# A flag for a second program: made from a value already in SBUF and loaded by the engines in the midst of the first program, in place of its end

## The chip, the cores and the metric

The kernel runs on one core of a Trainium2 chip, as one launch. The metric is the device time of that launch in microseconds; lower is better. The engines are TensorE (PE, with its weight loads shown apart as PEld), VectorE (DVE), ScalarE (ACT), GpSimd (POOL) and SyncE (SP). SP issues every DMA here. A row that ends in q (SPq, ACTq, PEldq) is an instruction that an engine's sequencer handles by itself: a wait, a register load, a jump, a DMA issue.

## The reference, cut to what matters

```python
scores = q @ k^T / sqrt(64)                  # 4 batches, 12 heads, 448 x 448
scores = cap * tanh(scores / cap)            # cap is an input, 30.0 here
attn   = softmax(scores)
x      = attn @ v                            # 1792 tokens x 768
h = x @ w_in;  x = (h * cos(h)) @ w_out      # 768 -> 2048 -> 768
a = x @ w1; b = x @ w2                       # 768 -> 1024, twice
out = ((a * b) @ w3) @ w_out2                # 1024 -> 1024 -> 768
```

## The kernel before

The kernel holds two programs that compute the same thing. The first, `program(...)`, takes the softmax without subtracting the maximum, which is safe only while |cap| is at most `CAP_MAX` = 40. The second, `program(..., general=True)`, subtracts the maximum. The first always runs; a flag `large` (1 when |cap| > 40) decides at run time whether the second runs after it and overwrites the output. With cap = 30 the flag is 0, and every engine jumps over the second program's instructions to the end of the code.

In each program a planner (`Plan.schedule`) takes operations with costs and due times and writes out one list of instructions for all engines, in the order of its own modelled time `t`; the five engines execute their part of that list in order. Attention comes first (lines 574, 584, 595), then the first MLP with its three-term products of high and low halves (lines 357 to 359, tiles `wih`, `woh`, `xh`, `gh`), then the second MLP (tiles `w12h`, `w34h`, `abh`) whose results leave through the tiles `ob` (three buffers) to `outT`.

The flag before: behind the first program, `tile_kernel` loads cap from HBM once more (line 299, tile `cap2`, shown as `cap`), takes its absolute value and compares it (lines 300 to 302, on DVE), and each of the five engines loads the flag from SBUF into a register (`nc.values_load`, line 303, a TENSOR_LOAD; SP adds a range check of two instructions, FUSED_REGOPS and SEQ_ASSERT). Then each engine executes the jump of `tc.If` (COMPARE_BRANCH, also line 303). These instructions are placed by the framework, not by the planner: each stands on its engine as soon as its inputs allow. In `program`, line 446 already makes `pac` = |cap| in SBUF at the start, on all 128 partitions.

Of the kernel before, what the change touches and what calls it, by code (L numbers as in the profile page):

```python
# [10 lines left out]
F32 = mybir.dt.float32  # L11
# [3 lines left out]
ALU = mybir.AluOpType  # L15
# [18 lines left out]
CAP_MAX = 40.0  # L34
# [255 lines left out]
def tile_kernel(tc, *args):  # L290


    nc = tc.nc
    cap = args[3]
    program(tc, *args)
    with tc.tile_pool(name="large", bufs=1) as p:
        c = p.tile([1, 2], F32, name="cap2")
        large = p.tile([1, 1], mybir.dt.int32, name="large")
        nc.sync.dma_start(c[:, 0:1], cap.rearrange("(o n) -> o n", o=1))
        nc.vector.tensor_scalar(c[:, 1:2], c[:, 0:1], -1.0, None, op0=ALU.mult)  # L300
        nc.vector.tensor_tensor(c[:, 0:1], c[:, 0:1], c[:, 1:2], op=ALU.max)
        nc.vector.tensor_scalar(large, c[:, 0:1], CAP_MAX, None, op0=ALU.is_gt)
        with tc.If(nc.values_load(large[0:1, 0:1], min_val=0, max_val=1) > 0):
            program(tc, *args, general=True)


@with_exitstack
def program(
# [12 lines left out]
    general=False,  # L321
):
    nc = tc.nc
    PE, ACT, DVE, POOL, SP = nc.tensor, nc.scalar, nc.vector, nc.gpsimd, nc.sync
    G = dict(PAR, **GENERAL) if general else PAR
    plan = Plan()
# [76 lines left out]
    def swap(*names, opens=()):  # L403


        def f():
            for n in names:
                pools[n].close()
            for n in opens:
                pools[n].open()  # L410

        plan.event(f, [pools[n] for n in names], [pools[n] for n in opens])
# [21 lines left out]
    def const(shape, name, dtype=F32):  # L434
        return pools["const"].pool.tile(shape, dtype, name=name, bufs=1)
# [8 lines left out]
    pac = const([P, 1], "pac")  # L444
# [5 lines left out]
    warm = const([P, 1], "warm")  # L450
    DVE.memset(warm, 0.0)
    ACT.activation(warm, warm, AF.Tanh)


    xh_r = ring("xring", "xh", [P, KD, S], F32R)
# [657 lines left out]
    swap("wp", opens=("yp", "mp", "cv"))  # L1113
    swap("cv", "attn", opens=("lp",))
    swap("mp", "yp", "wi", opens=("qp", "q2"))
    for _, f in plan.schedule():
        if f is not None:
            f()
    for n in ("q2", "qp", "lp", "psum", "dram", "xring", "const"):
        pools[n].close()  # L1120


# [40 lines left out]
```

## Time and profile before

| | us |
|---|---|
| time, median of three runs (lowest, highest) | 1142.9 (1142.64, 1143.47) |
| time of the profiled execution | 1141.23 |
| its span, first to last instruction | 1139.2 |
| PE busy | 1112.9 |
| DVE busy | 740.5 |
| ACT busy | 454.2 |
| POOL busy | 133.3 |

The span is what the trace covers; 2.03 us of the profiled execution's time lie outside it. PE is busy for 98% of the span, so its few gaps and the tail behind its last matmul are what is left beside its own work.

### The profile page before, as it was taken

The numbers are of one execution on the slowest core, as the hardware profiler recorded it, in microseconds if no ns is written. First come the engines' busy times: TensorE is split into PE (matmuls) and PEld (weight loads), VectorE is DVE, ScalarE is ACT, GpSimd is POOL, SyncE is SP. The second block draws the span as 40 slices with busy tenths as digits, with TensorE's granted clock in tenths as the row PEclk, the third lists the DMA queues.
The fourth block names the chain that finished last, engine by engine and source line by source line (L and its number), as shares of the span: only waits on it lengthen the run. The fifth ranks groups of instructions, "written<-read, shape, count | busy, mean of one in ns | idle before, by whom it ended". The sixth has DMA issues, their size and how long they took to land.

```text
span 1139.2 us, 13718 instructions
## 1 busy us (share of the span) xinstructions
PE 1112.9 (98%) x5184; PEld 966.5 (85%) x5184; DVE 740.5 (65%) x1111; ACT 454.2 (40%) x581; POOL 133.3 (12%) x130
## 2 busy tenths in 40 slices
PE   5999999999999999999999999999999999999997
PEld 3777777778888888889999999998999999999996
DVE  5888777899998897787899877768831311311111
ACT  4887767877566655722454211113211101101001
POOL 2312111123231110110121000001200000000000
PEclk9999999999999999999999999999999999999999
DMA  8885765878756554337745211101401101101001
GB/s 231 229 224 149 212 185 171 231 210 252 209 154 188 190 148 158 130 100 235 272 127 180 70 56 56 29 1 69 140 15 41 57 1 41 57 1 40 10 1 51
DMA packets 83165, 140.10 MB, mean 123 GB/s; under 512 B 35986, under 2 KB 63634, under 8 KB 83090
## 3 DMA queue, kind: packets, MB, share of 16 engines
q1 hardware_dynamic: 83090, 139.14, 40.7%
q8 instruction: 42, 0.69, 0.2%
q14 instruction: 33, 0.27, 0.1%
HBM read 109.45 MB, written 29.58 MB: 122 GB/s over the span
## 4 chain that ended last, share of the span: by engine, by line
PE 93%; DVE 2%; DMA 1%; ACT 1%; SPq 1%; issue 0%; POOL 0%; ACTq 0%; DVEq 0%
PE bank L357 13%; PE bank L358 13%; PE bank L359 13%; PE double L358 12%; PE double L359 12%; PE double L357 12%; PE bank L595 12%; PE double L574 3%; PE double L575 3%; DMA rawc<-in_w_out 1%; SPq L353 1%; DMA kr<-in_k 0%; DVE w L343 0%; ACT double L584 0%; ACT p L584 0%
## 5 line engine op out<-in xcount | busy, mean ns | idle before, releaser
L343 DVE TENSOR_TENSOR a<-double,a 128x448 f32<-128x448 f32 x32 | 20.0, 625 | 240.1 <-PE double L359 237.7
L595 PE MATMUL bank<-p,v 112*128 112x448 f32 x384 | 161.3, 543 | 0.5 <-issue 0.5
L359 PE MATMUL double<-xh,w12l 128*128 128x448 f32 x378 | 137.8, 365 | 0.0
L358 PE MATMUL double<-xl,w12h 128*128 128x448 f32 x378 | 137.8, 365 | 0.0
L357 PE MATMUL double<-xh,w12h 128*128 128x448 f32 x378 | 137.4, 363 | 0.0
L584 ACT ACTIVATE double<-double,ts 112x896 f32<-112x896 f32 x96 | 94.1, 981 | 79.1 <-PE double L575 78.9
L333 ACT COPY a<-double 128x448 f32<-128x448 f32 x31 | 16.5, 533 | 254.1 <-PE double L359 254.1
L357 PE MATMUL bank<-xh,wih 128*128 128x448 f32 x270 | 107.9, 399 | 0.0
L595 PEld LDWEIGHTS bank<-p,v 112*128 112x128 f32 x384 | 72.6, 190 | 41.2 <-issue 38.3
L357 PE MATMUL bank<-gh,woh 128*128 128x448 f32 x260 | 102.1, 393 | 0.3 <-ACT hs L333 0.3
L358 PE MATMUL bank<-xl,wih 128*128 128x448 f32 x270 | 98.3, 364 | 0.0
L359 PE MATMUL bank<-xh,wil 128*128 128x448 f32 x270 | 98.0, 363 | 0.0
L584 ACT ACTIVATE p<-double,pac 112x896 f32<-112x896 f32 x96 | 96.7, 1010 | 2.0
L358 PE MATMUL bank<-gl,woh 128*128 128x448 f32 x260 | 95.2, 366 | 0.0
L359 PE MATMUL bank<-gh,wol 128*128 128x448 f32 x260 | 94.8, 365 | 0.0
L574 PE MATMUL double<-qh,ks 128*112 128x448 f32 x192 | 73.7, 384 | 14.4 <-DVE ks L343 10.3
L343 DVE TENSOR_TENSOR y<-bank,y 128x448 f32<-128x448 f32 x111 | 68.6, 619 | 23.0 <-PE bank L359 22.2
L358 PEld LDWEIGHTS double<-xl,w12h 128*128 128x128 f32 x378 | 71.0, 188 | 5.8
L357 PEld LDWEIGHTS double<-xh,w12h 128*128 128x128 f32 x378 | 70.8, 187 | 5.6
L359 PEld LDWEIGHTS double<-xh,w12l 128*128 128x128 f32 x378 | 71.0, 188 | 5.0
L575 PE MATMUL double<-ql,ks 128*112 128x448 f32 x192 | 72.1, 375 | 0.0
L357 PEld LDWEIGHTS bank<-xh,wih 128*128 128x128 f32 x270 | 50.8, 188 | 9.0 <-issue 5.0
(153 smaller groups left out, 2359.2 us busy)
## 6 DMA issues: line engine op xcount, KB each, us to landing
rawc<-in_w_out SPq DMA_DIRECT2D x16, 768.0 KB, 5.6
rawl<-in_w SPq DMA_DIRECT2D x16, 768.0 KB, 4.4
qr<-in_q SPq DMA_DIRECT2D x48, 224.0 KB, 4.6
kr<-in_k SPq DMA_DIRECT2D x48, 224.0 KB, 4.9
rawc<-in_w_in SPq DMA_DIRECT2D x13, 768.0 KB, 5.0
raw<-in_w3T SPq DMA_DIRECT2D x16, 512.0 KB, 5.8
raw<-in_w_out SPq DMA_DIRECT2D x8, 768.0 KB, 7.2
wo_d<-wx SPq DMA_DIRECT2D x16, 384.0 KB, 4.4
```

Source lines behind the costliest of these rows:

```text
L333: "A": ("ACT", (0.051 if psum else 0.094) + n / 1200, lambda: ACT.copy(dst(), src())),
L343: "D": ("DVE", 0.068 + n / 960, lambda: DVE.tensor_tensor(dst(), a(), b(), op=op))
L353: plan.op(due, [("SP", 0.66, lambda: SP.dma_start(dst(), src()))], r=r, w=w, kb=kb)
L357: PE.matmul(out, wh, xh, start=first, stop=False)
L358: PE.matmul(out, wh, xl, start=False, stop=False)
L359: PE.matmul(out, wl, xh, start=False, stop=last)
L574: PE.matmul(o, w, qh(), start=True, stop=False)
L575: PE.matmul(o, w, ql(), start=False, stop=True)
L584: lambda f=f, x=x, o=o: ACT.activation(o(), s(), f, scale=x[:CP]))],
L595: PE.matmul(pv()[:, :S], w()[:, 2 * c + n].rearrange("p a d -> p (a d)"), p()[:, n, :], start=c == 0 and n == 0, stop=c == NT - 1 and n == 1)
```

## The change

The flag is now made inside the first program from `pac`, as an operation of the planner on DVE with due time 30 and cost 0.15. The five loads of the flag into registers are written out by hand at the first entry of the planner's list with modelled time over 600, and the register is handed back to the caller for the jump. The second load of cap, the absolute value and the tile `cap2` are gone. The jump itself stays where it was, at the end of the first program.

```diff
 def tile_kernel(tc, *args):
-    nc = tc.nc
-    cap = args[3]
-    program(tc, *args)
-    with tc.tile_pool(name="large", bufs=1) as p:
-        c = p.tile([1, 2], F32, name="cap2")
-        large = p.tile([1, 1], mybir.dt.int32, name="large")
-        nc.sync.dma_start(c[:, 0:1], cap.rearrange("(o n) -> o n", o=1))
-        nc.vector.tensor_scalar(c[:, 1:2], c[:, 0:1], -1.0, None, op0=ALU.mult)
-        nc.vector.tensor_tensor(c[:, 0:1], c[:, 0:1], c[:, 1:2], op=ALU.max)
-        nc.vector.tensor_scalar(large, c[:, 0:1], CAP_MAX, None, op0=ALU.is_gt)
-        with tc.If(nc.values_load(large[0:1, 0:1], min_val=0, max_val=1) > 0):
-            program(tc, *args, general=True)
+    with tc.If(program(tc, *args) > 0):
+        program(tc, *args, general=True)
...
     ACT.activation(warm, warm, AF.Tanh)
+
+    if not general:
+        large = const([1, 1], "large", mybir.dt.int32)
+
+        def is_large():
+            DVE.tensor_scalar(large, pac[0:1], CAP_MAX, None, op0=ALU.is_gt)
+
+        plan.op(30.0, [("DVE", 0.15, is_large)])
+    over = None
...
-    for _, f in plan.schedule():
+    for t, f in plan.schedule():
+        if over is None and not general and t > 600:
+            over = nc.values_load(large[0:1, 0:1], min_val=0, max_val=1)
         if f is not None:
             f()
...
+    return over
```

Apart from the rows of the flag, each engine's instructions keep their order. Three places show where those rows go.

ACT at the end of the first program, before. The three copies write the last output tiles; the last row is the first one of the second program.

```order
L333 COPY ob0_6106<-bank6_79 128x448
L333 COPY ob1_6112<-bank4_77 128x448
L333 COPY ob2_6119<-double1_76 128x448
L303 TENSOR_LOAD large_7571
L303 COMPARE_AND_BRANCH
L452 ACT_TABLE_LOAD
```

The same place now:

```order
L323 COPY ob0_6122<-bank6_79 128x448
L323 COPY ob1_6128<-bank4_77 128x448
L323 COPY ob2_6135<-double1_76 128x448
L293 COMPARE_AND_BRANCH
L442 ACT_TABLE_LOAD
```

The register load between the last copy and the jump is gone; PE and DVE lose theirs in the same way. On SP the load already stood far from the end before, behind the second load of cap.

SP in the first MLP, now. The DMAs fetch weights; ISA x2 is the range check. Before, the five DMAs above and the five below stood next to each other.

```order
L343 DMA wx1_1563<-wi_d_85 128x768
L343 DMA xl_1_3975<-w34_d_87 128x768
L343 DMA wx0_1542<-wo_d_86 128x768
L343 DMA rawl1_3847<-in_w12 128x1536
L343 DMA wx1_1563<-wo_d_86 128x768
L1117 TENSOR_LOAD large_103
L1117 ISA x2
L343 DMA wx0_1542<-wi_d_85 128x768
L343 DMA wx1_1563<-wi_d_85 128x768
L343 DMA rawl0_3838<-in_w12 128x1536
```

Three sequencer instructions moved in between the load of `wx1` from `wo_d` and that of `wx0` from `wi_d`.

PE at the same point of the list, now: a pair of products with `gh` ends, one with `xh` begins.

```order
L347 MATMUL bank7_80<-gh0_1635,woh3_1858 128x448
L348 MATMUL bank7_80<-gl0_1644,woh3_1858 128x448
L349 MATMUL bank7_80<-gh0_1635,wol3_1875 128x448
L1117 TENSOR_LOAD large_103
L347 MATMUL bank5_78<-xh0_438,wih2_1349 128x448
L348 MATMUL bank5_78<-xl0_454,wih2_1349 128x448
L349 MATMUL bank5_78<-xh0_438,wil2_1364 128x448
```

The load stands between two matmuls that followed one another before. In the trace of before this point is at 589.9 us, and it lies between 586 and 591 us on the other four engines.

## Rows read from the trace of the kernel before

**Rows 1.** The page's part 1: busy time, share of the span, instructions.

```profile
PE 1112.9 (98%) x5184; PEld 966.5 (85%) x5184; DVE 740.5 (65%) x1111; ACT 454.2 (40%) x581; POOL 133.3 (12%) x130
```

**Rows 2.** PE's waits: in total, times, longest us.

```profile
PE double L358 <- DVE gl L343: 2.6, 1, 2.6
```

**Rows 3.** Stretches: length, busy PE, PEld, DVE, ACT, POOL, granted clock, DMA, GB/s.

```profile
32.00:37.00 5.00, 5.00 (x16) 3.10 (x15) 4.97 (x9) 4.02 (x6) 1.25 (x1) 0.66 0.54 154
...
600.00:700.00 100.00, 100.00 (x496) 92.51 (x495) 82.06 (x131) 25.47 (x35) 7.50 (x6) 1.00 0.29 90
...
770.00:775.00 5.00, 2.42 (x13) 1.87 (x12) 4.55 (x8) 2.45 (x4) 0.00 (x0) 1.00 0.00 0
```

**Rows 4.** Line 303 from 1120 us: ns min/median/max, first and last start.

```profile
L303 SPq EVENT_SEMAPHORE  x8: 17/17/17, 1137.3 to 1137.8; - x8
...
L303 ACTq EVENT_SEMAPHORE  x2: 17/28/38, 1133.0 to 1136.7; - x2
...
L303 PEldq TENSOR_LOAD <-large x1: 490/490/490, 1127.5 to 1127.5; - x1
L303 PEldq COMPARE_BRANCH  x1: 3322/3322/3322, 1128.1 to 1128.1; - x1
L303 ACTq TENSOR_LOAD <-large x1: 550/550/550, 1133.1 to 1133.1; - x1
...
L303 SPq COMPARE_BRANCH  x1: 53/53/53, 1134.3 to 1134.3; - x1
```

**Rows 5.** Last matmul, a late copy on ACT, and the last output DMA.

```profile
1130.86 0.37 PE L359 MATMUL double<-abh,w34l 128*128 128x448 f32 x1
...
1131.62 1.11 ACT L333 COPY ob<-bank 128x448 f32<-128x448 f32 x2 [1.60 <-PEq L303]
...
L353 SPq DMA_DIRECT2D outT<-ob x1: 385/385/385, 1133.8 to 1133.8; - x1
...
DMA to landing us min/median/max: 2.8/2.8/2.8
```

**Rows 6.** Line 303 on SP in the middle of the program.

```profile
L303 SPq TENSOR_LOAD <-large x1: 702/702/702, 492.7 to 492.7; - x1
L303 SPq FUSED_REGOPS  x1: 188/188/188, 493.5 to 493.5; - x1
L303 SPq SEQ_ASSERT  x1: 37/37/37, 493.7 to 493.7; - x1
```

**Rows 7.** SP and DVE in order of time, 486 to 498 us (idle before, releaser).

```profile
486.26 0.45 SPq L299 DMA_DIRECT2D cap<-in_cap  x1
...
492.11 0.13 DVE L300 TENSOR_SCALAR cap<-cap 1x1 f32<-1x1 f32 x1
...
492.62 0.62 DVE L343 TENSOR_TENSOR y<-double,y 128x448 f32<-128x448 f32 x1
...
497.77 0.63 DVE L343 TENSOR_TENSOR y<-double,y 128x448 f32<-128x448 f32 x1 [1.73 <-PE double L359]
```

**Rows 8.** What stands behind the new loads: four engines, 588 to 592 us.

```profile
589.82 0.95 DVE L343 TENSOR_TENSOR wol<-wx,woh 128x768 fp32r<-128x768 f32 x1
...
589.93 0.96 ACT L959 ACTIVATE w<-w 128x896 f32<-128x896 f32 x1 [0.99 <-DVE w L343]
...
591.32 2.55 POOL L337 TENSOR_SCALAR woh<-wx 128x768 fp32r<-128x768 f32 x1 [4.71 <-DMA wx<-wo_d]
...
588.22 0.32 SPq L353 DMA_DIRECT2D wx<-wo_d  x1
590.80 6.88 SPq L353 DMA_DIRECT2D wx<-wi_d  x2
```

**Rows 9.** PE: a wait of its sequencer, and the matmul that it belongs to.

```profile
L357 PEldq EVENT_SEMAPHORE  x1: 51/51/51, 600.9 to 600.9; - x1
...
603.31 0.37 PE L357 MATMUL double<-gh,woh 128*128 128x448 f32 x1
```

**Rows 10.** DVE behind the arithmetic on cap at the start.

```profile
5.92 0.63 DVE L334 CAST qh<-qr 128x896 fp32r<-128x896 f32 x1 [1.66 <-DMA qr<-in_q]
```

## The prediction

> **What bounds the kernel now.** I read the busy shares first, then PE's waits, then the tail. PE is busy for 1112.9 of 1139.2 us [rows 1], so a change off PE's path can only act through a gap of PE or through the tail behind its last matmul. Inside the program the list of PE's waits has one large entry behind the start-up, 2.6 us on DVE's `gl` [rows 2], in the stretch 770 to 775 us, where DVE is busy for 4.55 of 5 us [rows 3]. The reader is to see that PE waits neither for SP nor for a flag anywhere.
>
> The tail decides this change. PE's last matmul runs from 1130.86 to 1131.23; the last output DMA is issued at 1133.8 and lands 2.8 us after that, at 1136.6 [rows 5]. SP jumps at 1134.3, as soon as that issue is done, and its next instruction, the first of eight waits, is at 1137.3 [rows 4]. Those 3.0 us are the jump: by then the DMA has been down for some 0.7 us. From there to the end of the span are 1.9 us of waits, one after another. So the tail hangs on SP: last issue, jump, waits.
>
> **The change part by part.** Everything is set against the profiled execution, 1141.23 us.
>
> *At the end.* PE, DVE and ACT lose their flag loads. On ACT the load takes 0.55 us from 1133.1, right behind the last copy's start, and ACT's own closing wait is over at 1136.7 [rows 4]; without the load and its dispatch ACT arrives some 0.6 us sooner, at 1136.1. It was not last: SP arrives at 1137.3. On PE the load takes 0.49 us at 1127.5 and the jump begins at 1128.1, while matmuls run until 1131.23 [rows 4, 5]; PE's jump lasts until 1131.4, and would again end about when the matmuls do. Gain at the end: 0. What is late next if I misread SP's 3.0 us is the landing of the last DMA, so the most that the tail can give is 1137.3 less 1136.6, 0.7 us.
>
> Would a flag known early make the jump itself cheap? The trace of before already holds that experiment. SP had its flag in a register from 493.7 us on [rows 6], because the framework had moved its load there, and still spent 3.0 us between its jump and the next instruction [rows 4]. ACT, PE and DVE only come to what SP had. The Trainium skill (Runtime: NRT & Kernel Launch, section Instruction fetch mechanics) gives a reason against the change: a taken branch to a target outside the instruction window must wait for a fetch of the target's page. By that rule the jump costs the same with an early flag, the sum has no term for it, and the trace agrees with its 3.0 us on SP. If instead the early flag let the jump be prepared, the sum would gain the 0.7 us above and no more.
>
> *At 486 to 494 us.* SP loses the issue of the second load of cap (0.45 us at 486.26) [rows 7] and a flag load with its range check: from 492.7 to 493.7, 0.70, 0.19 and 0.04 us with the gaps between them [rows 6]. DVE loses three tiny operations: from the first at 492.11 to the next real one at 492.62, 0.5 us. DVE then stands idle for 1.73 us before 497.77, waiting for PE [rows 7]; 0.5 us sooner it waits 0.5 us longer. Bounds: gain between 0 and 0.5 us. I take 0, because that idle time is three times the saving.
>
> *The flag made at the start.* One more DVE operation of a tenth or two of a us, like those on cap (0.13 us for a 1x1 tile [rows 7]). It stands in front of the first cast of `qh`, before which DVE idles for 1.66 us for a DMA [rows 10]. Cost 0; without that cover 0.2 us.
>
> *The five loads in the middle.* The dearest load in the trace is SP's 0.70 us, 1.05 us with its check [rows 6]. I go through what is queued behind each.
> - SP: the DMA in front is issued from 588.22 to 588.54, the one behind at 590.80 [rows 8]. The 1.05 us fit into 2.26 us; 1.2 us are left. The DMA behind waits for others, not for SP.
> - ACT: idle for 0.99 us before the `w` at 589.93, the load 0.55 us [rows 8, 4]. Hidden.
> - POOL: idle for 4.71 us before 591.32 [rows 8]. Hidden.
> - DVE: full there, with `wol` at 589.82 behind the load [rows 8]. At most 0.7 us lost, if the load can't run beside the operation in front. Over the next 100 us DVE is busy for 82 [rows 3], so 18 us can take it up before the one stretch where PE waits for DVE. Between 0 and 0.7 us on DVE; on PE's path I take 0.
> - PE: it is the one that matters, since PE has no idle time there. Its sequencer runs ahead of the array. The load at the end stands behind all matmuls in PE's order, and ran at 1127.5, when the last matmul was 3.4 us off [rows 4, 5]. Nearer to the new place, the wait at 600.9 belongs to the matmul at 603.31 (the only one of that stretch that waits for two engines): 2.4 us ahead [rows 9]. The load holds the sequencer for 0.6 us (1127.5 to 1128.1). Cost 0 with either lead; if the load emptied the array first, 0.6 us and the 0.37 us of a first matmul, 1.0 us. I take 0, since at the end the matmuls ran on beside the load.
>
> The Trainium skill (DMA: Bandwidth & Descriptors, section Latency and other measured facts) gives a floor of about 600 ns for such a register load. The trace has 490, 550 and 702 ns, so two of the three lie below that floor; by that figure the PE term would be the same 0 under a lead of 2.4 us, or 0.6 us if it were exposed.
>
> **Sum.** 0 at the end, 0 at 486 to 494, 0 at the start, 0 in the middle: 1141.23 us for an execution like the profiled one. It lies 1.67 us below the median of the three runs, 1142.9, so for the median I predict **1142.9 us**. Adding the bounds, the program can move between 1.2 us down (0.7 + 0.5) and 1.0 us up. About 0.2% of 1142.9, 2.3 us, is what a measurement of this kernel can tell from no change; neither bound reaches it.
>
> **The rivals.**
> - *The tail shortens* (0.08). For: ACT's copy at 1131.62 has 1.60 us of wait put down to PE's step on line 303 [rows 5], which would move with PE's load; and DVE's 0.5 us could survive. Against: that copy also needs the buffer of the first of six output DMAs, which were under way then. Gain 0.6 to 1.2 us: 1141.7 to 1142.3.
> - *PE waits for its load* (0.05). For: it is the first register load with matmuls behind it, and no row shows that. Against: rows 4 and 5. Cost up to 1.0 us: 1143.9.
> - *PE waits and loses its clock* (0.03), slower than before. After the start-up gaps the granted clock was 0.66 on average over 32 to 37 us, of its levels 2.4 and 1.2 GHz; that is 1.7 us of clock. Against: the 2.6 us gap at 771 was followed by no loss, the granted clock being 1.00 in 770 to 775 [rows 3]. 1.0 + 1.7 = 2.7 us: 1145.6. It decides as soon as the load empties the array and the clock follows once.
> - *The jump pays twice* (0.02): the code behind it lies elsewhere now, and a second wait like SP's 3.0 us would give 1145.9. Nothing in the rows speaks for it.
> - That the change doesn't do what it says is out: the order listing shows the loads where the diff puts them.
> - What I can't name, such as the buffers that lie 32 bytes further on because of the new tile: 0.05 faster and 0.02 slower by more than 0.2%.
>
> **How the numbers follow.** The forecast of no visible change has 0.75; with the first two rivals, which also stay within 0.2%, 0.88. Slower: 0.03 + 0.02 + 0.02 = 0.07. Faster: 0.05. Range: from the lowest run less the gains, 1142.64 - 1.2 = 1141.4, taken down to 1141.0 because the profiled execution itself had 1141.23; up to the highest run and the PE bound, 1143.47 + 1.0 = 1144.5. It leaves out the clock, the double jump and the unnamed, 0.12.
>
> **What the profile of the changed kernel would show.** Right: five TENSOR_LOADs between 586 and 592 us, PE's steps around 590 unbroken, SP's DMA behind its load still at 590.8; no ops of lines 300 to 302 at 492 and a DVE wait before 497.8 that is longer by 0.5 us; at the end ACT's closing wait 0.6 us earlier, SP's jump still followed by 3.0 us. Wrong: a step between two of PE's matmuls of 0.6 us or more at 590, a granted clock under 1.00 behind it, or SP's first wait at the end coming less than 2.5 us after its jump.

## The result, and the profile after

The changed kernel takes 1151.1 us in the median of six runs (1148.6 to 1153.2), against 1143.2 us for the kernel before (six runs, 1142.6 to 1146.1): a ratio of 1.006, with a 95% interval from 1.0045 to 1.0076. It is slower by 7 to 8 us, outside the predicted 1141.0 to 1144.5. The profiled execution has a time of 1148.61 us and a span of 1146.6, 7.4 us more than before.

Nothing that the change was said to touch carries that. The page's part 1 of the changed kernel, to be read against [rows 1]: the same 5184 matmuls, and PE is busy for 7.0 us more, while DVE and ACT have the same busy time within 0.4 us.

```profile
PE 1119.9 (98%) x5184; PEld 967.3 (84%) x5184; DVE 740.7 (65%) x1109; ACT 453.8 (40%) x581; POOL 135.2 (12%) x130
```

PE's largest wait inside the program is the one of [rows 2] still. The list of PE's waits, after:

```profile
PE double L348 <- DVE gl L333: 2.6, 1, 2.6
```

So PE doesn't wait longer; it works longer. Where, a table by stretches shows (length, busy us of PE, PEld, DVE, ACT, POOL with the number of instructions that started, granted clock, DMA share, GB/s). Two stretches in which PE never rests, one in the first MLP and one in the second, and two in which the clock moved (before, 32 to 37 us is in [rows 3]). Before:

```profile
500.00:580.00 80.00, 80.00 (x397) 74.21 (x396) 69.11 (x104) 27.42 (x39) 10.50 (x10) 1.00 0.67 223
770.00:785.00 15.00, 12.42 (x61) 10.98 (x60) 13.46 (x24) 6.02 (x10) 0.00 (x0) 1.00 0.00 0
800.00:1100.00 300.00, 300.00 (x1485) 278.39 (x1484) 76.72 (x123) 34.41 (x61) 6.73 (x6) 1.00 0.11 38
```

After:

```profile
32.00:37.00 5.00, 5.00 (x20) 3.40 (x19) 4.97 (x9) 4.97 (x7) 1.25 (x1) 1.00 0.61 203
500.00:580.00 80.00, 80.00 (x392) 73.34 (x391) 68.62 (x103) 26.97 (x39) 9.26 (x9) 1.00 0.67 220
770.00:785.00 15.00, 12.40 (x54) 11.02 (x54) 12.21 (x22) 5.40 (x9) 0.00 (x0) 0.89 0.00 0
800.00:1100.00 300.00, 300.00 (x1471) 276.28 (x1470) 79.89 (x127) 36.24 (x64) 7.79 (x7) 1.00 0.12 40
```

The reader divides length by matmuls. From 500 to 580 us a matmul takes 80/397 = 0.2015 us before and 80/392 = 0.2041 after; from 800 to 1100 us 300/1485 = 0.2020 and 300/1471 = 0.2039. PE is at 100% in all four and the granted clock is 1.00 in all four. Each matmul has become about 1% longer, with no gap between them. The two stretches stand on either side of the new register loads at 590 us, and the first lies before them, so those loads can't be the cause.

Matching the start of every matmul with that of its counterpart places the 7.4 us. At 206 us, where the first MLP's matmuls set in, the changed kernel is 1.8 us ahead; in 32 to 37 us alone it gained 1.7 us, because its clock did not fall there (1.00 above, 0.66 in [rows 3]). From there to 767 us it loses 5.0 us in small, even steps; 1.2 us around 778 us, where its clock fell (0.89) and that of before did not; 3.3 us in even steps to the last matmul; and the tail is 0.3 us shorter. The even steps are 8.3 us. The two clock events are of opposite sign and cancel for the greater part.

What the prediction did follow is unharmed. The new loads, by line:

```profile
L1117 POOLq TENSOR_LOAD <-large x1: 503/503/503, 587.1 to 587.1; - x1
L1117 PEldq TENSOR_LOAD <-large x1: 488/488/488, 587.9 to 587.9; - x1
L1117 ACTq TENSOR_LOAD <-large x1: 462/462/462, 589.3 to 589.3; - x1
L1117 DVEq TENSOR_LOAD <-large x1: 546/546/546, 590.2 to 590.2; - x1
L1117 SPq TENSOR_LOAD <-large x1: 488/488/488, 590.3 to 590.3; - x1
```

PE in order of time at the place of its load, which stands between the first two of these rows in PE's order:

```profile
591.32 0.36 PE L349 MATMUL bank<-gh,wol 128*128 128x448 f32 x1
591.52 0.37 PE L347 MATMUL bank<-xh,wih 128*128 128x448 f32 x1
591.73 0.37 PE L348 MATMUL bank<-xl,wih 128*128 128x448 f32 x1
```

The load ran at 587.9, 3.6 us before the matmul behind it at 591.52, and the steps around it are 0.20 and 0.21 us. On SP the load fits in front of a DMA that comes no later for it:

```profile
589.89 0.32 SPq L343 DMA_DIRECT2D wx<-wo_d  x1
592.47 6.89 SPq L343 DMA_DIRECT2D wx<-wi_d  x2
```

From the end of the first to the second are 2.26 us, as in [rows 8] to the hundredth. The tail, by line (answers to [rows 4]):

```profile
L293 SPq EVENT_SEMAPHORE  x8: 17/17/17, 1144.7 to 1145.2; - x8
...
L293 SPq COMPARE_BRANCH  x1: 50/50/50, 1141.7 to 1141.7; - x1
L293 ACTq EVENT_SEMAPHORE  x1: 17/17/17, 1142.6 to 1142.6; - x1
```

SP's jump at 1141.7 is followed by the first wait at 1144.7: 3.0 us, as before, and ACT, without its load, is done 2.1 us before SP (0.6 us before it in [rows 4]).

### The profile page after: what moved, and what is told of

It is laid out like the page before. It is cut to its first block, busy times and chain, and to the rows that moved or that the text cites. A ratio compares the mean times of both kernels' runs of the same rounds, so it can differ in the third digit from the quotient of the medians.

```text
span 1146.6 us, 13710 instructions
## 1 busy us (share of the span) xinstructions
PE 1119.9 (98%) x5184; PEld 967.3 (84%) x5184; DVE 740.7 (65%) x1109; ACT 453.8 (40%) x581; POOL 135.2 (12%) x130
## 4 chain that ended last, share of the span: by engine, by line
PE 92%; DVE 2%; DMA 2%; ACT 1%; issue 0%; SPq 0%; ACTq 0%; DVEq 0%
PE bank L347 13%; PE bank L349 13%; PE bank L348 13%; PE double L349 12%; PE double L348 12%; PE double L347 12%; PE bank L594 11%; PE double L573 3%; PE double L574 3%; DMA raw<-in_w_out 2%; DMA kr<-in_k 1%; DVE w L333 0%; ACT double L583 0%; SPq L343 0%; DVE y L333 0%
## 5 line engine op out<-in xcount | busy, mean ns | idle before, releaser
L348 PEld LDWEIGHTS bank<-xl,wih 128*128 128x128 f32 x270 | 50.9, 188 | 9.2 <-issue 5.2
```

The lines of the kernel that those rows point to most:

```text
L348: PE.matmul(out, wh, xl, start=False, stop=False)
```

## The experiments

The suspects were three. **A:** the flag's tile takes 32 bytes in the first pool of SBUF, and 53 buffers behind it, among them `xh` and `xl`, which stream through PE as moving operands in both MLPs, lie 32 bytes further on; their place changes the matmul's step. **B:** the register loads or the flag's DVE operation cost the time. **C:** the clock's fall behind the gap at 771 us.

**Only the 32 bytes.** The kernel before, with

```diff
     warm = const([P, 1], "warm")
+    if not general:
+        const([P, 1], "pad")
```

> The kernel before, with nothing of the change but one unused 32-byte tile at the place in SBUF where the change puts its flag, so that the same 53 buffers lie 32 bytes further on. Theory A (the place of the buffers makes PE's matmuls slower): 1149 to 1152 us, ratio to before 1.005 to 1.007, and a step between PE's matmuls of 0.205 us in the stretch from 500 to 580 us, where before has 0.202. Theory B (the register loads in the middle, or the flag made at the start, cost it): 1143 us, ratio 1.000. Theory C (PE's clock fell once behind the gap near 771 us): 1143 us or, if it falls here too, 1.2 us more.

Measured: 1153.1 us, ratio 1.0076 (1.0051 to 1.0102). An unused tile alone costs as much as the change did, within the two intervals; the time is 1 us above the range expected. Its stretches:

```profile
500.00:580.00 80.00, 80.00 (x392) 73.25 (x391) 68.20 (x104) 26.24 (x38) 9.30 (x9) 1.00 0.64 216
800.00:1100.00 300.00, 300.00 (x1472) 275.97 (x1471) 79.37 (x126) 36.27 (x64) 7.62 (x7) 1.00 0.13 44
```

392 and 1472 matmuls, as in the changed kernel (392, 1471).

**The change without the 32 bytes.** The changed kernel, with the flag in the second word of the tile `warm`, which takes 32 bytes anyway:

```diff
-    warm = const([P, 1], "warm")
+    warm2 = const([P, 2], "warm")
+    warm = warm2[:, 0:1]
...
-        large = const([1, 1], "large", mybir.dt.int32)
+        large = warm2[0:1, 1:2].bitcast(mybir.dt.int32)
```

> The change in full, but the flag lies in the unused second word of the 32 bytes that the tile named warm already takes, so that every other buffer has the address that it had before. Theory A: 1143 us, ratio 1.000 (0.998 to 1.002), PE's steps 0.202 us from 500 to 580 us. Theory B: 1149 to 1152 us, ratio 1.006. Theory C: 1143 us, with no tie to the addresses.

Measured: 1143.8 us, ratio 0.9995 (0.9982 to 1.0007).

```profile
500.00:580.00 80.00, 80.00 (x397) 74.22 (x396) 68.90 (x105) 27.10 (x39) 9.69 (x9) 1.00 0.66 218
770.00:785.00 15.00, 12.39 (x54) 11.03 (x53) 12.15 (x21) 5.17 (x9) 0.00 (x0) 0.89 0.00 0
800.00:1100.00 300.00, 300.00 (x1485) 278.36 (x1484) 79.24 (x126) 35.44 (x62) 7.21 (x7) 1.00 0.12 38
```

397 and 1485: the counts of before. All of the change's instructions are in it, and it costs nothing that can be measured. B falls. C falls with it: the clock fell behind the gap near 771 us in this profile too (0.89 in the second row), and the time is that of before.

**64 bytes.** The changed kernel with the `pad` tile of the first experiment as well.

> The change in full with one more unused 32-byte tile behind the flag, so that the 53 buffers lie 64 bytes further on than before. Theory A with a period of 64 bytes (only the remainder by 64 counts, and it is 32 for all buffers, as before): 1143 us, ratio 1.000. Theory A with a longer period or none: another time, 1145 us or more. Theory B: 1149 to 1152 us, as the changed kernel.

Measured: 1148.3 us, ratio 1.0040 (1.0024 to 1.0057). Not the time of before: the remainder by 64 is not all that counts.

**32 bytes above xh and xl.** The kernel before, with a pool of 32 bytes opened between the pool of `xh` and `xl` and that of attention:

```diff
-    for n in ("const", "xring", "dram", "psum", "attn", "wi", "wp"):
+    for n in ("const", "xring", "gap", "dram", "psum", "attn", "wi", "wp"):
         pools[n].open()
+    pools["gap"].pool.tile([P, 1], F32, name="pad", bufs=1)
```

> The kernel before with 32 unused bytes between the buffers of xh and xl and those of attention and of the early weights of the second MLP: xh and xl stay where they were, the attention buffers and the early w12 and w34 tiles move by 32 bytes. Theory A, if it is the place of xh and xl as the moving operand that counts: 1143 us, ratio 0.999 to 1.001, steps of 0.202 us from 500 to 580 us. Theory A, if it is the place of the attention buffers and the early weights: up to 1150 us. Theory B: 1143 us.

Measured: 1143.0 us, ratio 0.999 (0.9976 to 1.0004). The attention buffers and early weights moved, `xh` and `xl` did not, and the time stayed. So it is the four buffers of `xh` and `xl`; what remained was whether their place counts by itself (A1) or against that of the weights, which PE's weight loads read while the moving operand streams (A2; in the stretch from 500 to 580 us of before, PEld is busy for 74 us beside PE's 80).

**The other side moved instead.** The buffers that grow from the far end of SBUF (`wi`, `wo`, `g`, `y`, most of `w12` and `w34`) were moved by a pool opened first on that side:

```diff
-    for n in ("const", "xring", "dram", "psum", "attn", "wi", "wp"):
+    for n in ("const", "xring", "dram", "psum", "attn", "rgap", "wi", "wp"):
         pools[n].open()
+        if n == "rgap":
+            pools[n].pool.tile([P, 8], F32, name="pad_r", bufs=1)
```

> The kernel before, with xh, xl and all buffers of attention in place, and the buffers on the other side of SBUF (wi, wo, g, y, most of w12 and w34) moved by 32 bytes the other way, so that xh lies 32 bytes further from its weights, as in the changed kernel. Theory A1 (the absolute place of xh and xl counts): 1143 us, ratio 0.998 to 1.002, steps of 0.202 us from 500 to 580 us. Theory A2 (the place of xh and xl relative to the weights that are loaded beside them counts): 1149 to 1153 us, ratio 1.005 to 1.008, steps of 0.205 us.

Measured: 1153.1 us, ratio 1.0080 (1.0063 to 1.0098). `xh` stands exactly where it stood before, and the kernel is as slow as with the pad in front of it.

```profile
500.00:580.00 80.00, 80.00 (x391) 73.23 (x390) 66.58 (x102) 25.99 (x37) 9.40 (x9) 1.00 0.65 217
800.00:1100.00 300.00, 300.00 (x1463) 274.45 (x1462) 78.44 (x125) 36.11 (x63) 8.44 (x7) 1.00 0.13 43
```

**Both sides, 256 bytes in sum.** The pad of 32 bytes of the first experiment, and the pool on the far side with 224 bytes (56 words in place of 8).

> The kernel before with xh, xl and the attention buffers moved by 32 bytes, as in the changed kernel, and the other side moved by 224 bytes the other way, so that the distance between the two grows by 256 bytes. Theory A1 (absolute place): 1149 to 1153 us, ratio 1.005 to 1.008, steps of 0.205 us. Theory A2 with a period that divides 256 bytes: 1143 us, ratio 0.998 to 1.002, steps of 0.202 us; A2 with a longer period: in between or slower.

Measured: 1142.1 us, ratio 0.9984 (0.9971 to 0.9996). `xh` lies where it lies in the changed kernel, and the slowness is gone. A1 falls, and A2 fits all six experiments so far: the distance counts, and 256 bytes more leave it as it was.

```profile
500.00:580.00 80.00, 80.00 (x398) 74.26 (x397) 68.89 (x105) 27.20 (x39) 9.66 (x9) 1.00 0.65 218
800.00:1100.00 300.00, 300.00 (x1485) 278.58 (x1484) 79.74 (x127) 35.32 (x62) 7.75 (x7) 1.00 0.11 38
```

**96 and 128 bytes.** The pad of the first experiment with 24 and with 32 words in place of one.

> The kernel before with 96 unused bytes in front of xh. With 32 bytes the ratio was 1.0076, with 64 (beside the flag) 1.0040. Both forms of theory A with a period of 64 bytes are out already; with a period of 128, 96 bytes is the one offset not yet seen, and any value from 0.998 to 1.010 fits. If the steps depend on the place only through whole multiples of 64 or not, 1150 us as with 32 bytes.

> The kernel before with 128 unused bytes in front of xh. Theory A with a period of 128 bytes (or 32 or 64): 1143 us, ratio 0.998 to 1.002. With a longer period: another time, as 32 and 64 bytes gave.

Measured: 1151.0 us, ratio 1.0060 (1.0041 to 1.0080), and 1147.8 us, ratio 1.0036 (1.0021 to 1.0050). A period of 128 bytes is out as well.

**What the traces of these runs say of the distance.** For each matmul of the MLPs behind attention (from about 495 us on) I took the address of its moving operand and that of the weights loaded next, from the built programs, and their difference modulo 256 bytes. The mean step to the next matmul, by that difference (number of pairs in brackets):

```
difference   0              64            96            128           160           192
before       0.2039 (1716)  0.2021 (151)                                            0.2007 (1241)
changed      0.2040 (1709)                0.2015 (151)                0.2056 (1241)
64 bytes     0.2050 (1709)                              0.2035 (1392)
96 bytes     0.2041 (1718)                0.2062 (1241)               0.2054 (151)
128 bytes    0.2056 (1706)  0.2018 (1241)                                           0.2002 (151)
```

The 1241 pairs of before at 192 are those of `xh` with the weights on the far side. The change put them at 160, the slowest column but one. Where 192 occurs, it is the best column of its row. In the kernel before, more than half of the pairs lie at 0, so there was something to be had.

A pair's own distance is not the whole of it. By the table, with 128 bytes some 1.4 us of the loss come from the large group (192 to 64), but some 2.9 us from the pairs at 0, whose distance did not change. The means at 0 are good to about 0.001 us (0.2031 in the second experiment, which has the addresses of before), so this is more than scatter. Most plainly, the 430 products of `abh` and `abl` with `w34` on the far side, where neither operand moved, step by 0.2057 us there, and by 0.2026 in the kernel before and in the three others with its distances (no shift, both sides, and the last one below). And the 151 pairs at 96 step by 0.2015 us in the changed kernel but by 0.2062 with the other side moved instead, at the same distance. What else these steps depend on is open.

A rival that needs no new run is that the moved buffers collide with other engines or with DMAs. Between 800 and 1125 us, 400 of the 583 pairs at 192 of before ran while DVE, ACT and POOL did nothing and no DMA packet was under way, and so did 380 of the 553 pairs at 160 of the changed kernel. Their mean steps are 0.2003 and 0.2053 us, the same as those of all such pairs there. So the cost is there without any work of the others.

**Every pair at 192.** The flag in the unused word, as in the second experiment, a gap of 192 bytes as in the fourth, and `g` and `ab` placed 64 bytes further inside buffers that are 256 bytes larger:

```diff
+    class Shifted(Ring):
+        def tile(self, k):
+            if k not in self.tiles:
+                n = math.prod(self.shape[1:])
+                t = self.pool.pool.tile([P, n + 64], ...)[:, 16:16 + n]
...
-        g_r = hl("mp", "g", [P, 2, S], 2)
+        g_r = [Shifted(plan, pools["mp"], "g" + x, [P, 2, S], F32R, 2) for x in "hl"]
...
-        ab_r = hl("qp", "ab", [P, S], 2)
+        ab_r = [Shifted(plan, pools["qp"], "ab" + x, [P, S], F32R, 2) for x in "hl"]
```

> The changed kernel with the flag in a word that was unused, and with pads that put every moving operand of both MLPs (xh, xl, g, ab) at the same distance from its weights, 192 bytes modulo 256: a gap of 192 bytes below the attention buffers and early weights, and 64 bytes inside the g and ab buffers. Before, 2122 of 3967 such pairs of matmul and next weight load lay at 0 and stepped by 0.2036 to 0.2043 us, 1694 at 192 with 0.2003 to 0.2011. Theory A2 (the distance counts): some 1006 x 0.0033 + 694 x 0.0032 + 420 x 0.002 = 6 us less than before, 1137 to 1139 us, ratio 0.993 to 0.997, steps under 0.2025 us in both MLPs. If the slow steps of xh come from something else that the pads only happened to move: 1142 to 1144 us or, with the moved g and ab in other bad places, more.

Measured: 1135.1 us, ratio 0.9931 (0.9919 to 0.9944): 8 us less than before, with the change's loads in it and as many instructions as the changed kernel. It is faster than both kernels. The ratio lies in the range expected, the time 2 us below it; the spans of the two profiled executions differ by 6.1 us (1133.1 against 1139.2), which is what the sum had.

```profile
PE 1106.2 (98%) x5184; PEld 967.0 (85%) x5184; DVE 743.7 (66%) x1109; ACT 453.8 (40%) x581; POOL 133.1 (12%) x130
...
500.00:580.00 80.00, 80.00 (x402) 74.84 (x401) 69.70 (x105) 27.85 (x41) 10.52 (x10) 1.00 0.68 225
800.00:1100.00 300.00, 300.00 (x1502) 281.19 (x1501) 76.37 (x123) 35.01 (x62) 6.79 (x6) 1.00 0.11 38
```

402 and 1502 matmuls in the stretches where before had 397 and 1485; 300/1502 = 0.1997 us each.

**The change as it is, with the distance mended.** The changed kernel, flag tile included, and the far side moved by 224 bytes.

> The changed kernel as it is, flag tile and register loads included, with only the buffers of the other side moved by 224 bytes the other way, so that the 32 bytes of the flag become 256 in the distance. Theory A2: 1143 us, ratio 0.997 to 1.001. If the change has a cost of its own beside the distance: more than 1144.5 us, ratio over 1.001.

Measured: 1142.8 us, ratio 0.9992 (0.9983 to 1.0002). The flag tile may stay where it is, if the far side follows.

## Why the prediction was wrong

The step that failed is the prediction's first premise, that a change off PE's path "can only act through a gap of PE or through the tail", and with it a term that the sum does not have. The prediction names it, "the buffers that lie 32 bytes further on because of the new tile", among the things that I could not name a price for, gives it 0.02 for a loss over 0.2%, and leaves it out of the parts of the change. It was the whole result: the first experiment costs 0.76% with that tile alone, the second and the last show the rest of the change at -0.05% and -0.08%, with intervals from -0.18% to 0.07%. What would have warned me was in the trace of before: matmuls of one form that step by different times at a granted clock of 1.00, which no wait explains. In the second MLP the 216 products of `xh` with a `w12h` on the far side step by 0.199 us, the 168 with one of the early `w12h` by 0.204. I read PE as busy at 98% and took its busy time as fixed by the work.

The rest, by its steps:

- *End: gain 0.* Right. SP's jump kept its 3.0 us, and no other engine was later than SP. ACT's arrival moved further ahead of SP's than I said, by 1.5 us in place of 0.6, and it moved nothing. The tail is 0.3 us shorter, within the bound of 0.7.
- *486 to 494 us: gain 0.* Right in size, but not where I put it. DVE's 0.5 us did not lengthen the wait before [rows 7]'s last operation, which stayed (1.75 us, 1.73 before); DVE met a wait of its own at once. DVE in order of time, after:

```profile
493.07 0.62 DVE L333 TENSOR_TENSOR y<-double,y 128x448 f32<-128x448 f32 x1 [0.48 <-PE double L349]
...
498.25 0.62 DVE L333 TENSOR_TENSOR y<-double,y 128x448 f32<-128x448 f32 x1 [1.75 <-PE double L349]
```

- *The loads in the middle: cost 0.* Right on all five engines. PE's lead was 3.6 us, more than the 2.4 I counted on, and the dearest load in the middle took 0.55 us, not the 0.70 taken as the bound.
- *Rivals.* None of them happened as written. "PE waits and loses its clock" ended on the right side for a wrong reason: PE did not wait for its load. Its "against", that the gap at 771 us costs no clock, does not hold: in 8 of the 12 kernels profiled here the clock was halved for 3.4 us or more some microseconds behind that gap, in kernels fast and slow alike. Six of the eight falls began behind 775 us, where the row that I read ends; the one profiled execution of the kernel before has none.
- *Range.* Its bounds were those of the waits that I had listed, and so could not hold a cost that sits in PE's busy time.

What stays open is why the distance counts. The runs show that moving the stream against the weights beside it makes the cost and takes it away again, and the mean steps at 0, 64, 96, 128, 160 and 192 bytes modulo 256. They do not separate the weights that are loaded next from those in use, since for nearly all pairs both lie at the same distance here, and they do not show why pairs that kept their distance can change their step too. 32 and 224 were not tried for the large group; in the fourth experiment 569 other pairs lie at 32 and step by 0.2037 us.

## What to carry to other kernels

A new tile, however small, can move every buffer allocated behind it (here 53); compare the addresses of both programs as well as the order of their instructions before calling an edit free. Where PE is full, count matmuls per microsecond in a stretch without gaps: a step that differs between two stretches of the same shape at the same granted clock may be room to gain or to lose. An unused tile added to the kernel before, and the change without its shift, are two cheap runs that tell the place from the instructions.

## What the runs showed of the hardware that was not expected

- In an unbroken stream at a granted clock of 1.00, the mean step from one 128x448 matmul to the next went from 0.200 to 0.206 us with the distance, modulo 256 bytes, between its moving operand and its weights in SBUF, though not with that alone. All pairs at 192: 0.1997 us from 800 to 1100 us; with the large group at 160 in place of 192: 0.2039 to 0.2051. Over this kernel that is from 1135 to 1153 us, 1.6%, with the same 5184 matmuls.
- The granted clock can fall to half for 3.4 us (in one case 6.8) behind a gap of PE of 2.6 us or not, from one profiled execution to the next: 0.89 over 770 to 785 us in the changed kernel, 1.00 in the kernel before, with the same gap in both.
- A jump over the second program costs 3.0 us on SP whether its register was loaded 640 us before (kernel before) or 551 us before (after): the load is not what it waits for. What it does wait for, no run here shows.
